# Two shifted copies of VectorE's exponentials in one instruction, in a kernel of two attention and two linear-attention layers

## The chip, the cores and the metric

The kernel runs on one core of a Trainium2 chip. A core has TensorE (PE, matrix multiplications into PSUM), VectorE (DVE), ScalarE (ACT), GpSimd (POOL), SyncE (SP, which here issues DMAs), an SBUF of 128 partitions and a PSUM of eight banks of 128x512 fp32. Each engine works through its own list of instructions in order and waits on semaphores for the others. The metric is the device time of one execution in microseconds (us), lower is better.

## What is computed

Four residual layers on one sequence of 2048 tokens of width 512, alternating between two kinds. Kind A is softmax attention with 32 query heads of width 16 and a single key and value head; kind B is linear attention with a feature map of exp.

```python
x = A_x                                             # 2048 x 512, bf16
x = x + A(layernorm(x), wq, wk, wv, wo)             # layer 0
x = x + B(layernorm(x), wqkv, wo)                   # layer 1
x = x + A(layernorm(x), wq, wk, wv, wo)             # layer 2, the weights of layer 0
x = x + B(layernorm(x), wqkv, wo)                   # layer 3, the weights of layer 1

A: scores = q k^T / 4;  p = softmax(scores);  out = (p v) wo
B: phi(t) = (t + 1 if t > 0 else exp(t)) + 1e-6
   o = phi(q) (phi(k)^T v) / (phi(q) sum(phi(k)) + 1e-6);  out = o wo
```

An A layer needs 32 x 2048 x 2048 exponentials, and these fill most of the time.

## The kernel before

**Tiles and segments.** Tokens come in 16 tiles of 128. In an A layer the work is cut into blocks: one block is the scores of 128 keys against 512 columns (a query tile of 128 tokens for four heads), which is one PSUM bank. A segment (`Seg`) is half of one query tile's heads against a range of key tiles; a layer has 2048 blocks in all. For each block TensorE makes the scores (L965, tile `ps<-QT,KM`, a matmul that uses 32 of the 128 rows, so that up to four run side by side), an engine takes the exponential out of PSUM into SBUF, and TensorE multiplies it by the values (L1019) into 32 columns of the accumulator bank `ACC`; four blocks of different column groups run side by side as one value group.

**Two engines take exponentials.** ScalarE takes the exact one (L1150, tile `PT`) of two or three banks at a time. There are two bank sets of three banks each: while ScalarE works on one, TensorE fills the other. VectorE takes an approximation (L1247, tile `FB`): scores come out of TensorE scaled so that adding a constant and writing as int16 gives the bits of a bf16 power of two. That is piecewise linear, and it is made smooth by averaging: the same bits plus 32, 64 and 96 (a quarter, a half and three quarters of an octave) make three more copies (L1289), and each of the four copies (`NSH = 4`) is multiplied with its own weighted values (`VW`, weights `WTS`). So a block of ScalarE's costs TensorE one value matmul, and a block of VectorE's costs four, plus its share of three copies on VectorE.

**Chunks and buffers.** VectorE collects up to `CHB = 4` blocks in one buffer of `FB`, a chunk of 2048 elements in each partition; `dve_close` then starts `dve_shifts`, which takes three more buffers, one after the other, and posts a copy for each. `FB` has 12 buffers (`NFB`). A buffer comes free when the copies that read it and the value matmuls on it are done (`hold`, `spend`). A new chunk is opened only with more than `FBO` buffers free (`dve_hit`), and a copy for a segment that isn't due yet waits while no more than `FBS` are free.

**Who gets a block.** A block goes to VectorE in one of three ways: as the third bank of a round (`dve_split`; ScalarE then takes two banks, and the set is given back when both engines are done with it), if VectorE has less than `BLS` us queued of some urgency and less than `BLT` in all; in a free bank beside a round (`dve_open`); or by itself when VectorE runs low (`alone`).

**The order.** No order is written by hand. A planner (`Planner`) runs the whole program once in Python, while the kernel is built, with an assumed duration and latency for every operation, and gives each engine the ready operation of the best priority whenever it is free. What comes out is a fixed list for each engine, with semaphore waits; only the lists run on the chip. The assumed durations are in the `op(...)` calls and in constants (`PV_DUR` 0.222 for a value group, `QK_LAT` 0.438 from the start of score matmuls to the exponential, `SWITCH` 0.107 between row and column use of TensorE, `EXO` 0.0625 plus 0.4267 a bank for an exponential, `EX_LAT` 0.185 from its end to whoever waits for it). One rule concerns TensorE: `yields` (L72 to L78) holds back an operation that isn't a score matmul when it would make the next score matmuls of a set late. `self.turns` has for each running exponential when it will be done and how late the score matmuls into its banks may start; an operation is held if it would end more than `HTOL` + `HK` x (time until the banks are free) after the later of the two. Where TensorE would be empty, `fill` (L1064) puts in matmuls on zeros.

```python
            if r < self.now + HMAX and self.now + dur - max(r, late()) > HTOL + HK * max(0.0, r - self.now):
                return max(r, self.now) + 0.005
```

```python
BLS = 1.6        # L428
FBO = 2          # L455
FBS = 4          # L456
HTOL = 0.02      # L485
```

Of the kernel before, what the change touches and what calls it, by code (L numbers as in the profile page):

```python
# [8 lines left out]
I16 = mybir.dt.int16  # L9
ACTF = mybir.ActivationFunctionType  # L10
ALU = mybir.AluOpType
# [413 lines left out]
FARO = 12  # L425
FARM = {1: range(4, 16), 3: ()}
GROW = (5,)
BLS = 1.6  # L428
BLO = 5.0
DXB = 1.4  # L430
BLT = 2.5
# [16 lines left out]
NSH = 4  # L448
WTS = (0.353515625, 0.296875, 0.25, 0.2099609375)
WLOG = 0.5565237382  # L450
EXPBIAS = (SHIFT + WLOG) * math.log(2.0)
VB = (127.0 + SHIFT) * 128.0
VLO = 16384.0
CHB = 4
FBO = 2  # L455
FBS = 4  # L456
AHEAD = 20
QUICK = (4, 12)
KFIRST = True
# [22 lines left out]
OWNP = 2.0  # L482
HMAX = 0.2
KSP = True
HTOL = 0.02  # L485
HK = 0.3
MCOP = (DV,)*4
EVP = 1.2
# [8 lines left out]
def bass_interleave_layers__grouped_kv_mqa__linear_attn_block__prompt_kernel(  # L497
# [458 lines left out]
    def run_a(L):  # L956
# [13 lines left out]
        def pv_post(src, blk, hold, w=None):  # L970
            def arrived():
                for sg, kt, j, ap, key in blk:
                    sg.ready.append((kt, j, ap, key, hold, w))
                pv_kick()
            if src.done:
                arrived()
            else:
                src.users.append(arrived)

        def spend(h, o):  # L980
            h[0] -= 1
            if o not in h[1]:
                h[1].append(o)
            if h[0] == 0:
                pl.give_after(h[2], h[3], h[1])
# [233 lines left out]
        def dve_hit(js):  # L1219
            if not chunk["blk"] and (len(fb_pool.free) <= FBO or fb_pool.wait):  # L1220
                return None
            hit = dve_pick(js)
            if hit is not None:
                if not chunk["blk"]:
                    chunk["f"] = fb_pool.free.pop(0)
                    chunk["hold"] = [NSH - 1, [], fb_pool, chunk["f"]]
                hit[0].need[hit[2]] += NSH - 1
                hit[0].total += NSH - 1
            return hit
# [43 lines left out]
            pl.process(dve_shifts(blk, chunk["f"], chunk["hold"]))  # L1273

        def dve_shifts(blk, f_, hold):
            n = 512 * len(blk)
            pr = 8.0 + 0.001 * min(x[0].i for x in blk)
            si = min(x[0].i for x in blk)
            for w in range(1, NSH):
                while len(fb_pool.free) <= FBS and sum(x.total - x.submitted for x in segs[cur["i"]:si]) > (AHEAD if segs[si].blocks < 32 else 0):  # L1280
                    yield ("sleep", 0.2)
                g_ = yield ("acq", fb_pool, pr)
                while PSH and len(blk) == CHB and pl.backlog(DV) > PBL and not all(o.done for o in pl.ws(("FB", f_, len(blk) - 1))):
                    yield ("sleep", 0.1)
                pool = PSH and len(blk) == CHB and not pl.busy[PO] and state["po"] == 0 and pl.backlog(DV) > PBL
                if pool:
                    state["po"] += 1
                en, du = (PO, n / 1165.0 + 0.25) if pool else (DV, n / 3840.0 + 0.068)
                o = op({en: (du, lambda e, w=w, g_=g_: e.tensor_scalar(  # L1289
                    out=FB[:, g_, 0:n].bitcast(I16), in0=FB[:, f_, 0:n].bitcast(I16), scalar1=float(w * 128 // NSH), scalar2=None, op0=ALU.add))},  # L1290
                       reads=[("FB", f_, h) for h in range(len(blk))], writes=[("FB", g_, h) for h in range(len(blk))], prio=pr, lat=0.15, port=True)
                if pool:
                    def gone():
                        state["po"] -= 1
                    o.users.append(gone)
                spend(hold, o)
                pv_post(o, [(sg, kt, j, FB[:, g_, h * 512:(h + 1) * 512], ("FB", g_, h)) for h, (sg, kt, j) in enumerate(blk)], [len(blk), [], fb_pool, g_], w)

        oslot = {}

# [581 lines left out]
```

## Time and profile before

| | us |
|---|---|
| median of three runs | 1488.83 (1487.35 to 1489.05) |
| the profiled execution | 1489.33 |
| its span, first instruction to last | 1487.6 |
| TensorE busy | 1433.2 (96%) |
| VectorE busy | 1439.2 (97%) |
| ScalarE busy | 1452.5 (98%) |

The views used are: the page's busy time of each engine; the chain of waits (followed back from the last instruction, at each step to what released it); the costliest groups of instructions (line, engine, operation, tile written <- tiles read, shapes, count | busy us, mean ns of one | idle time before them and what ended it); the waits (engine and line that waited <- what it waited for: us in total, times, longest); and the order of instructions in time (start, duration, engine, line; neighbours of one line are merged, with their count). A record lasts until its result is written and so overlaps the next record of its engine; the cost of an instruction to its queue is the distance from its start to the next one's. PEld is the loading of weights into TensorE, which a matmul starts with. The first A layer runs its exponentials from about 10 to 707 us, the second from about 700 to 1451 us, with layer 1 mostly between and beside them, and layer 3 at the end.

### The profile page before, as it was taken

The page shows a single profiled execution, that of the slowest core. Times are in us where ns is not written, and L with a number is a line of the kernel's source. Part 1 is how long each engine was busy: PE and PEld are TensorE (multiplying, and loading weights), DVE is VectorE, ACT ScalarE, POOL GpSimd, SP SyncE. Part 2 cuts the span into 40 slices and gives each one's busy share as a digit, 9 for nine tenths or more (in the row PEclk, how much of TensorE's full clock was granted, in tenths as well). Part 3 has the DMA queues.
Part 4 walks back from the last instruction along what each step waited for, and adds up shares of the span by engine and source line. Part 5 has one row for each costly group of instructions (what it writes and reads, how often), then busy time and mean ns, then how long its engine had stood idle before and what let it go on. Part 6 is the DMA issues. An engine that isn't in the chain of part 4 may idle for free.

```text
span 1487.6 us, 36547 instructions
## 1 busy us (share of the span) xinstructions
PE 1433.2 (96%) x14825; PEld 520.1 (35%) x14924; DVE 1439.2 (97%) x2686; ACT 1452.5 (98%) x1444; POOL 77.0 (5%) x155
## 2 busy tenths in 40 slices
PE   8999999999999999999999999999999999999998
PEld 5423333333333333333733333333333333333335
DVE  8999999999999999999878999999999999999996
ACT  8999999999999999999799999999999999999996
POOL 5000000000000000000011000000000000000000
PEclk9999999999999999999999999999999999999999
DMA  5200000000000000000031000000000000000001
GB/s 115 72 9 9 9 8 7 6 7 6 9 9 9 9 5 5 2 2 2 2 47 40 2 12 9 12 9 5 8 9 5 9 9 9 9 2 2 2 2 58
DMA packets 53542, 20.74 MB, mean 14 GB/s; under 512 B 47232, under 2 KB 52864, under 8 KB 53376
## 3 DMA queue, kind: packets, MB, share of 16 engines
q1 hardware_dynamic: 52320, 18.36, 5.7%
q8 instruction: 120, 1.97, 0.6%
q14 instruction: 46, 0.38, 0.1%
q10 hardware_dynamic: 1056, 0.03, 0.0%
HBM read 5.28 MB, written 2.10 MB: 5 GB/s over the span
## 4 chain that ended last, share of the span: by engine, by line
DVE 46%; PE 38%; ACT 7%; issue 7%; DMA 1%; POOL 0%; POOLq 0%; SPq 0%; ACTq 0%
DVE FB L1247 22%; DVE FB L1289 16%; PE ps L1019 13%; PE ps L965 11%; ACT PT L1150 7%; PE ps L711 5%; PE ps L1064 4%; PE ps L879 2%; PE ps L1334 1%; DVE sacc L1312 1%; DVE st L793 1%; DVE xn L802 1%; DVE QT L1422 1%; DVE Osb L1345 1%; DVE sacc L1422 1%
## 5 line engine op out<-in xcount | busy, mean ns | idle before, releaser
L1150 ACT ACTIVATE PT<-ps 128x1024 bf16<-128x1024 f32 (+1 forms) x1309 | 1400.1, 1309 | 5.6 <-PE ps L1019 2.7
L1247 DVE TENSOR_SCALAR FB<-ps 128x512 int16<-128x512 f32 x1047 | 689.0, 680 | 4.4 <-PE ps L965 3.1
L965 PE MATMUL ps<-QT,KM 32*128 32x512 bf16 x4096 | 525.6, 385 | 24.9 <-ACT PT L1150 16.9
L1019 PE MATMUL ps<-FB,VW 128*32 128x512 bf16 x4188 | 526.1, 384 | 8.3 <-DVE sacc L1312 5.3
L1289 DVE TENSOR_SCALAR FB<-FB 128x2048 int16<-128x2048 int16 (+1 forms) x789 | 517.6, 676 | 0.3
L1019 PE MATMUL ps<-PT,V 128*32 128x512 bf16 x3049 | 472.8, 386 | 0.4 <-issue 0.3
L965 PEld LDWEIGHTS ps<-QT,KM 32*128 32x128 bf16 x4096 | 133.0, 91 | 466.5 <-ACT PT L1150 381.7
L1064 PE MATMUL ps<-QT,V 128*32 128x512 bf16 (+6 forms) x927 | 249.8, 347 | 0.4
L1019 PEld LDWEIGHTS ps<-FB,VW 128*32 128x32 bf16 x4188 | 130.4, 94 | 163.3 <-issue 97.1
L1019 PEld LDWEIGHTS ps<-PT,V 128*32 128x32 bf16 x3049 | 114.7, 94 | 102.9 <-issue 74.5
L1064 PEld LDWEIGHTS ps<-QT,V 128*32 128x32 bf16 x927 | 79.8, 96 | 88.6 <-issue 32.9
L784 POOL TENSOR_TENSOR rs<-ve,mhalf 128x1 f32<-128x1 f32 x59 | 43.9, 745 | 578.9 <-DVE ve L782 576.6
L711 PE MATMUL ps<-wqkv,xnT 128*128 128x512 bf16 (+1 forms) x217 | 62.2, 367 | 7.0 <-issue 3.5
L1419 ACT ACTIVATE phE<-ps 128x512 bf16<-128x512 f32 (+1 forms) x66 | 45.8, 696 | 6.0 <-PE ps L879 5.0
L782 POOL TENSOR_SCALAR ve<-mv 128x1 f32<-128x1 f32 x32 | 14.9, 466 | 683.8 <-DVE mv L794 683.7
L1312 DVE COPY sacc<-ps 128x512 f32<-128x512 f32 x64 | 43.6, 681 | 3.3 <-PE ps L1019 3.2
L1334 PE MATMUL ps<-identF,sacc 128*128 128x128 f32 x256 | 46.3, 291 | 0.0
L793 DVE BATCH_NORM_STATS2 st<-x_sb 128x6 f32<-128x512 bf16 x60 | 40.5, 681 | 2.5 <-DMA x_sb<-in_A_x_dram 2.3
L879 PE MATMUL ps<-xnT,wqkv 128*128 128x128 bf16 x512 | 38.0, 220 | 0.0
L879 PE MATMUL ps<-xnT,wq 128*128 128x128 bf16 x464 | 35.2, 220 | 0.0
L1334 PEld LDWEIGHTS ps<-identF,sacc 128*128 128x128 f32 x256 | 27.3, 140 | 20.6 <-issue 11.8
L879 PEld LDWEIGHTS ps<-xnT,wqkv 128*128 128x128 bf16 x512 | 29.5, 98 | 9.8 <-issue 7.0
(139 smaller groups left out, 630.4 us busy)
## 6 DMA issues: line engine op xcount, KB each, us to landing
out_dram<-x_sb SPq DMA_DIRECT2D x16, 128.0 KB, 1.7
x_sb<-in_A_x_dram SPq DMA_DIRECT2D x6, 256.0 KB, 5.0
wqkv<-in_B_wqkv_dram SPq DMA_DIRECT2D x1, 1536.0 KB, 8.7
xnT<-xn SPq DMA_TRANSPOSE x48, 2.4
x_sb<-in_A_x_dram SPq DMA_DIRECT2D x4, 128.0 KB, 2.4
wq<-in_A_wq_dram SPq DMA_DIRECT2D x1, 512.0 KB, 4.5
wo<-in_A_wo_dram SPq DMA_DIRECT2D x1, 512.0 KB, 5.4
wo<-in_B_wo_dram SPq DMA_DIRECT2D x1, 512.0 KB, 9.4
```

The source lines that it names most:

```text
L711: return e.matmul(dst, lhsT=l, rhs=r, start=(k == 0), stop=(k == len(pairs) - 1))
L793: op({DV: (0.6, lambda e: e.bn_stats(st[:, t, 0, :], x_sb[:, t, :]))}, reads=[("x", t)], writes=[("st", t)], prio=prio, lat=0.13)
L879: ins = e.matmul(dst[:, g * P:(g + 1) * P], lhsT=lhs(g, k), rhs=rhs(k), start=(k == 0), stop=(k == FT - 1))
L965: return e.matmul(bank(b), lhsT=KM[r, sg.par, kt * P:(kt + 1) * P], rhs=QT[r, sg.t, :], start=True, stop=True)
L1019: ins = e.matmul(ps[32 * j:32 * j + 32, ACC * 512:(ACC + 1) * 512], lhsT=V[:, kt, :] if w is None else VW[:, kt, w, :], rhs=ap, start=(k = ...
L1064: o = op({PE: (n / 2400.0, lambda e: e.matmul(ps[32 * j:32 * j + 32, b * 512:b * 512 + n], lhsT=V0[:], rhs=QT[:, sg.t, 0:n], start=st, sto ...
L1150: ex = op({AC: (EXO + 0.4267 * n, lambda e, n=n, s_=s_, p_=p_: e.activation(PT[:, p_, 0:n * 512], ps[:, s_ * 512:(s_ + n) * 512], ACTF.Exp ...
L1247: o = op({DV: (0.602, lambda e: e.tensor_scalar(out=dst.bitcast(I16), in0=bank(b), scalar1=VB, scalar2=VLO, op0=ALU.add, op1=ALU.max))}, w ...
L1289: o = op({en: (du, lambda e, w=w, g_=g_: e.tensor_scalar(out=FB[:, g_, 0:n].bitcast(I16), in0=FB[:, f_, 0:n].bitcast(I16), scalar1=float(w ...
L1312: o = op({DV: (0.6, lambda e, src=src: e.tensor_copy(src, bank(ACC)))}, writes=[B_(ACC), key], prio=0.0, lat=0.15)
L1334: o = op({PE: (0.12, lambda e, c=c: e.transpose(ps[:, b * 512 + c * P:b * 512 + (c + 1) * P], src[:, c * P:(c + 1) * P], identF[:]))}, rea ...
L1419: op({AC: (0.07 + n / 1200.0, lambda e: e.activation(phE[:, i, 0:n], bank(b, n), ACTF.Exp))}, reads=[B_(b)], writes=[("phE", i)], prio=pr ...
```

## The change

The three copies of a chunk were three instructions, each reading the chunk's own buffer. Now the first instruction makes the copy shifted by one step (32) into a buffer `a_`, and a second instruction reads the two buffers `f_` and `a_` together, adds two steps (64), and writes two buffers `b_` and `c_`: the copies shifted by two and by three steps. The pattern over two buffers is a slice with a step, `FB[:, lo:hi + 1:hi - lo, 0:n]`, so the two need not be neighbours. Both `f_` and `a_` are held until this instruction is done, and `b_` and `c_` are taken at the same time. `wait` replaces the acquisition by priority: it polls every 0.1 us of the planner's time until enough buffers are free. An unused way to put copies on GpSimd (`PSH`) goes. Four constants change with it.

```diff
-BLS = 1.6
+BLS = 1.2
...
-FBO = 2
-FBS = 4
+FBO = 3
+FBS = 2
...
-HTOL = 0.02
+HTOL = .05
...
-                    chunk["hold"] = [NSH - 1, [], fb_pool, chunk["f"]]
+                    chunk["hold"] = [1, [], fb_pool, chunk["f"]]
...
-            for w in range(1, NSH):
-                while len(fb_pool.free) <= FBS and sum(x.total - x.submitted for x in segs[cur["i"]:si]) > (AHEAD if segs[si].blocks < 32 else 0):
-                    yield ("sleep", 0.2)
-                g_ = yield ("acq", fb_pool, pr)
...
-                en, du = (PO, n / 1165.0 + 0.25) if pool else (DV, n / 3840.0 + 0.068)
-                o = op({en: (du, lambda e, w=w, g_=g_: e.tensor_scalar(
-                    out=FB[:, g_, 0:n].bitcast(I16), in0=FB[:, f_, 0:n].bitcast(I16), scalar1=float(w * 128 // NSH), scalar2=None, op0=ALU.add))},
-                       reads=[("FB", f_, h) for h in range(len(blk))], writes=[("FB", g_, h) for h in range(len(blk))], prio=pr, lat=0.15, port=True)
...
-                spend(hold, o)
-                pv_post(o, [(sg, kt, j, FB[:, g_, h * 512:(h + 1) * 512], ("FB", g_, h)) for h, (sg, kt, j) in enumerate(blk)], [len(blk), [], fb_pool, g_], w)
+            def wait(least):
+                return len(fb_pool.free) < least or fb_pool.wait or (len(fb_pool.free) < least + FBS and
+                       sum(x.total - x.submitted for x in segs[cur["i"]:si]) > (AHEAD if segs[si].blocks < 32 else 0))
...
+            def add(out, in_, c, k, reads, writes):
+                return op({DV: (k * n / 3840.0 + 0.068, lambda e: e.tensor_scalar(out=out.bitcast(I16), in0=in_.bitcast(I16), scalar1=float(c * 128 // NSH), scalar2=None, op0=ALU.add))},
+                          reads=[("FB", g, h) for g in reads for h in range(m)], writes=[("FB", g, h) for g in writes for h in range(m)], prio=pr, lat=0.15, port=True)
+
+            while wait(1):
+                yield ("sleep", 0.1)
+            a_ = fb_pool.free.pop(0)
+            o = add(FB[:, a_, 0:n], FB[:, f_, 0:n], 1, 1, [f_], [a_])
+            held = [m + 1, [], fb_pool, a_]
+            pv_post(o, [(sg, kt, j, FB[:, a_, h * 512:(h + 1) * 512], ("FB", a_, h)) for h, (sg, kt, j) in enumerate(blk)], held, 1)
+            while wait(2):
+                yield ("sleep", 0.1)
+            b_, c_ = sorted(fb_pool.free[0:2])
+            fb_pool.free = fb_pool.free[2:]
+            lo, hi = min(a_, f_), max(a_, f_)
+            o = add(FB[:, b_:c_ + 1:c_ - b_, 0:n], FB[:, lo:hi + 1:hi - lo, 0:n], 2, 2, [f_, a_], [b_, c_])
+            spend(hold, o)
+            spend(held, o)
+            post(o, b_, 2 if f_ == lo else 3)
+            post(o, c_, 3 if f_ == lo else 2)
```

More of the change, by code (lines that the diff above doesn't have):

```diff
@@ L451 @@
 EXPBIAS = (SHIFT + WLOG) * math.log(2.0)
+assert NSH == 4
 VB = (127.0 + SHIFT) * 128.0
@@ L1275, in dve_shifts @@
         def dve_shifts(blk, f_, hold):
[L1276 to L1277 removed]
+            m = len(blk)
+            n = 512 * m
             si = min(x[0].i for x in blk)
[L1279 to L1297 removed]
```

3 lines of the change are left out of this document (added).

## The prediction

> **What bounds the kernel now.** I read the page first: busy shares, then the chain of waits, then the costliest groups.
>
> ```profile
> span 1487.6 us, 36547 instructions
> PE 1433.2 (96%) x14825; PEld 520.1 (35%) x14924; DVE 1439.2 (97%) x2686; ACT 1452.5 (98%) x1444; POOL 77.0 (5%) x155
> DVE 46%; PE 38%; ACT 7%; issue 7%; DMA 1%; POOL 0%; POOLq 0%; SPq 0%; ACTq 0%
> L1150 ACT ACTIVATE PT<-ps 128x1024 bf16<-128x1024 f32 (+1 forms) x1309 | 1400.1, 1309 | 5.6 <-PE ps L1019 2.7
> L1247 DVE TENSOR_SCALAR FB<-ps 128x512 int16<-128x512 f32 x1047 | 689.0, 680 | 4.4 <-PE ps L965 3.1
> L1289 DVE TENSOR_SCALAR FB<-FB 128x2048 int16<-128x2048 int16 (+1 forms) x789 | 517.6, 676 | 0.3
> L1064 PE MATMUL ps<-QT,V 128*32 128x512 bf16 (+6 forms) x927 | 249.8, 347 | 0.4
> ```
>
> Three engines are full. L1247 and L1289 are VectorE's exponentials and their shifted copies; L1150 is ScalarE's exponentials; L1064 is filler that TensorE runs when nothing else is wanted, so TensorE has room and the other two have little. The chain passes through VectorE far more often than through ScalarE, so VectorE looks like the engine to relieve. The chain of the first attention layer's steady part (100 to 700 us) and of the second's (765 to 1440 us) say the same:
>
> ```profile
> by line: DVE FB L1247 26.4%; DVE FB L1289 19.0%; PE ps L1019 14.6%; PE ps L965 11.7%; ACT PT L1150 7.0%; PE ps L1064 4.9%; issue 3.1%; PE ps L711 2.8%; DVE sacc L1312 1.9%; PE ps L1334 1.8%; DVE sacc L1422 0.8%; DVE va L705 0.8%; DVE Osb L1
> by line: DVE FB L1247 22.5%; DVE FB L1289 16.5%; PE ps L1019 12.5%; PE ps L965 11.1%; issue 10.6%; ACT PT L1150 6.7%; PE ps L1064 4.0%; PE ps L711 3.8%; DVE sacc L1312 1.1%; PE ps L879 1.0%; PE ps L1334 1.0%; DVE QT L1422 1.0%; DVE Osb L134
> ```
>
> But "7%" does not mean that ScalarE has time to spare. Records overlap their successors, so the cost of one instruction is the distance between starts, which the order of instructions in time shows (ScalarE alone, then VectorE alone; the row at 1449.91 is a piece of the chain of waits):
>
> ```profile
> 938.31 5.60 ACT L1150 ACTIVATE PT<-ps 128x1024 bf16<-128x1024 f32 x6
> 943.73 0.67 ACT L1419 ACTIVATE phE<-ps 128x512 bf16<-128x512 f32 x1
> 944.21 1.11 ACT L1150 ACTIVATE PT<-ps 128x1024 bf16<-128x1024 f32 x1
> ...
> 1448.58 4.32 ACT L1150 ACTIVATE PT<-ps 128x1536 bf16<-128x1536 f32 x3
> 1449.91 3.00 ACT PT L1150 x2
> ...
> 699.90 1.28 DVE L1289 TENSOR_SCALAR FB<-FB 128x2048 int16<-128x2048 int16 x2
> 701.10 1.28 DVE L1247 TENSOR_SCALAR FB<-ps 128x512 int16<-128x512 f32 x2
> 702.30 0.28 DVE L1420 TENSOR_SCALAR phE<-phE 128x512 bf16<-128x512 bf16 x1
> 702.50 0.68 DVE L1289 TENSOR_SCALAR FB<-FB 128x2048 int16<-128x2048 int16 x1
> ```
>
> A two-bank exponential costs (943.73 - 938.31)/6 = 0.903 us, a three-bank one 1449.91 - 1448.58 = 1.33, a 512-column one 944.21 - 943.73 = 0.48. VectorE's exponential and its 2048-element copy cost 0.60 each, a 512-element one of the same kind 0.20.
>
> ```profile
> L1150 ACT ACTIVATE PT<-ps 128x1024 bf16<-128x1024 f32 x371 | 377.7, 1174 | 0.3 <-PE ps L1019 0.3
> L1150 ACT ACTIVATE PT<-ps 128x1536 bf16<-128x1536 f32 x186 | 282.0, 1594 | 0.4 <-PE ps L1019 0.4
> L1419 ACT ACTIVATE phE<-ps 128x512 bf16<-128x512 f32 x19 | 13.6, 716 | 0.0
> L1150 ACT ACTIVATE PT<-ps 128x1024 bf16<-128x1024 f32 x432 | 434.4, 1180 | 0.3 <-PE ps L965 0.3
> L1150 ACT ACTIVATE PT<-ps 128x1536 bf16<-128x1536 f32 x196 | 296.4, 1593 | 1.3 <-PE ps L1019 1.3
> L1419 ACT ACTIVATE phE<-ps 128x512 bf16<-128x512 f32 x29 | 22.0, 759 | 0.2 <-DVE FB L1289 0.2
> ```
>
> These groups are the two steady parts, 600 and 675 us. ScalarE's starts alone need 371x0.903 + 186x1.33 + 19x0.48 = 591.5 us of the first and 432x0.903 + 196x1.33 + 29x0.48 = 664.7 us of the second. That leaves 8.5 and 10.3: in 1275 us ScalarE loses about 19 us, 1.5%. Nothing can shorten these parts by more, unless ScalarE gets less to do.
>
> **The change part by part.** The changed instruction lists count differently, because the planner decides anew.
>
> *VectorE.* From 0.60 and 0.20 a copy costs 0.26 ns an element and 0.067 us fixed. A copy of two buffers (4096 elements) then costs 1.133; the bounds are 1.133 (all of one fixed part saved) and 1.20 (nothing saved), and I take 1.133, since 512 and 2048 lie on one line. The list has 259 copies of 2048 and 259 of two buffers in place of 777: 466.2 - 259x(0.60 + 1.133) = 17.4 us less. Short chunks: nine copies of 1536 (0.466 by the same line) and three of 1024 (0.333) become one of 0.333 and one of 0.60, 4.3 less. Exponentials: 1038 for 1047, 5.4 less. Together VectorE sheds 27.1 us. On the chain these two lines have about 42% of the time (45.4% and 39.0% above), so the end would move by 0.42x27.1 = 11.4 us at most; the rest lies beside ScalarE and TensorE.
>
> Of 259 copies of two buffers 92 lie in adjacent buffers on both sides, and 167 go row by row (two rows of 2048). No instruction of this trace reads two rows at this rate. [...] The second copy reads what the first has just written and waits for it; only where the two follow directly is VectorE idle for that, some 40 places in the list by what precedes each, well under 0.1 us each, and I count nothing, as VectorE now has 27 us to hide it in.
>
> A longer instruction makes what comes behind it on VectorE wait up to 1.13 instead of 0.60, above all the emptying of the value accumulator (L1312), and TensorE's next value group behind that. The filler covers it on TensorE; without cover it is half of 0.53 at 64 places times the share of such copies in VectorE's time (about a fifth), some 3 us. I leave it at nothing and keep it in the range.
>
> *Buffers and gates.* A chunk now takes its last two buffers at once (of 12), holds its first two until the double copy, and opens only with more than 3 free (FBO 3); BLS 1.2 lets VectorE take the third bank of a round only with less queued. That is why it gets 9 blocks fewer, and ScalarE more: 894 two-bank and 423 three-bank exponentials and one of a single bank, for 878 and 431: 16x0.903 - 8x1.33 + 0.48 = +4.3 us on ScalarE. Nothing hides that but the 19 us. The finer polls (0.1) issue no instruction, and SP, POOL and the DMAs keep their lists.
>
> *HTOL, 0.02 to 0.05.* This is the part that I weigh most. `yields` holds back a value group that would delay the next score matmuls of a bank set beyond HTOL. By its own constants, a value group (0.222) that starts when an exponential is done (EX_LAT 0.185), with a two-bank exponential running on the other set, makes these matmuls late by 0.185 + 0.222 - (0.0625 + 0.8534 - 0.438 - 0.107) = 0.036: refused before, allowed now. The lists show it. Before, 10 rounds of score matmuls stand directly behind a value group that reads the exponential which also frees their banks, 6 of them with a two-bank exponential running; now 199 do, 123 with two banks running. What one costs the trace of before shows, since some happen there:
>
> ```profile
> PEld ps L1019 <- ACT PT L1150: 4.9, 12, 0.7
> ...
> 1363.11 1.11 ACT L1150 ACTIVATE PT<-ps 128x1024 bf16<-128x1024 f32 x1
> 1364.27 0.10 PEld L1019 LDWEIGHTS ps<-PT,V 128*32 128x32 bf16 x4 [0.29 <-ACT PT L1150]
> 1364.60 0.39 PE L965 MATMUL ps<-QT,KM 32*128 32x512 bf16 x4
> 1364.03 1.10 ACT L1150 ACTIVATE PT<-ps 128x1024 bf16<-128x1024 f32 x1
> 1365.05 1.45 ACT L1150 ACTIVATE PT<-ps 128x1536 bf16<-128x1536 f32 x1
> ...
> 16.26 1.06 ACT L1150 ACTIVATE PT<-ps 128x1024 bf16<-128x1024 f32 x1
> 17.21 1.45 ACT L1150 ACTIVATE PT<-ps 128x1536 bf16<-128x1536 f32 x1
> ...
> 1433.41 1.27 ACT L1150 ACTIVATE PT<-ps 128x1024 bf16<-128x1024 f32 x1
> 1434.58 1.02 ACT L1150 ACTIVATE PT<-ps 128x1024 bf16<-128x1024 f32 x1
> ```
>
> The exponential ends at 1364.22, the value group loads at 1364.27, the score matmuls follow 0.33 later, and ScalarE's next start is 1.02 after the last one instead of 0.903: 0.12 lost. Nine rounds of before have this shape; the first loses 0.05, the last 0.27, their mean is 0.15. Of the 19 us, other two-bank rounds lose 0.02 each. So 123 - 6 = 117 more rounds cost ScalarE 117x(0.15 - 0.02) = +15.2 us, against 0.036 in the planner's sum. Bounds: 117x(0.05 - 0.02) = 3.5 and 117x(0.27 - 0.02) = 29; I take the mean of the nine. Behind the waiting value group stand the score matmuls, and ScalarE waits for those: what was beside the path lies on it.
>
> *The sum.* ScalarE +4.3 + 15.2 = +19.5; VectorE's relief takes 11.4 off the waits in which ScalarE and TensorE stood behind VectorE: +8.1. The profiled execution took 1489.33 (its span of 1487.6 and 1.7 around it) and would take 1497.4; against the median shown, 1488.83, it is 1496.9, and I say 1497.
>
> **The rivals.** *VectorE is the bound and its relief wins.* The chain (46% to 7%) speaks for it, and so does the filler: the changed list has 868 for 927, 384,512 columns for 399,488, as if the planner found less empty TensorE time. It needs the value-first rounds to cost what the planner thinks, 117x0.036 = 4.2 us and that inside ScalarE's 19. Then -11.4 + 4.3 = -7.1: 1482. Against it: the nine rounds.
>
> *ScalarE's queue sets the whole end.* If VectorE's relief frees nothing that ScalarE waited for, all +19.5 stays: 1508. The point from which it decides: more than 15 us of before's 19 must be waits for TensorE, not VectorE. For it, the waits view: of the score matmuls' waits few end on VectorE,
>
> ```profile
> PEld ps L965 <- ACT PT L1150: 381.7, 1023, 1.2
> PEld ps L965 <- DVE FB L1247: 46.2, 115, 0.6
> ```
>
> against it, that value groups are late because their VectorE blocks were.
>
> *It cancels.* At half the price of a value-first round (7.6) the sum is 4.3 + 7.6 - 11.4 = +0.5: 1489.
>
> *The double copy doesn't run at the fast rate.* At half of it the 167 two-row copies cost 4096x0.52 ns + 0.067 = 2.2, 1.07 more each, +178 us: 1667. Only a new access pattern speaks for it; it is left outside the range.
>
> **How the numbers follow.** Forecast (slower, about 1497) 0.50; the full queue 0.13; cancels 0.12; VectorE's relief wins 0.23; slow mode 0.02. About 0.2%, 3 us, is what this kernel's measurement can tell from no change. Faster by more is the relief, 0.23; within is the cancelling, 0.12; slower is the rest, 0.65. The forecast's own range is 1491 to 1504 (half and one and a half of 15.2). The range for 8 in 10 reaches to the relief and to the full queue: 1481 to 1509.
>
> **What would show it.** Right: the two-buffer copy's starts 1.13 apart, VectorE with some 2% idle and well under 46% of the chain, ScalarE with more; value groups that wait for ScalarE some 200 times and not 12, and two-bank exponentials 0.15 apart from their floor behind them. Wrong: ScalarE's loss in the steady parts falls below 19 us, which would mean that a value-first round is absorbed by a round before it that was late too; or a double copy above 1.2.

## The result, and the profile after

| kernel | median of runs, us | profiled span, us | ratio to before, 95% interval |
|---|---|---|---|
| before | 1488.84 (1487.35 to 1489.05, 4 runs) | 1487.6 | |
| changed | 1498.12 (1497.25 to 1498.15, 4 runs) | 1496.4 | 1.0062 [1.0050, 1.0075] |

The changed kernel is 9.3 us slower, 1.1 over the forecast of 1497. The page of the changed kernel, in the parts shown of before (the last two lines are groups with shapes kept apart):

```profile
span 1496.4 us, 36075 instructions
PE 1440.3 (96%) x14752; PEld 519.5 (35%) x14842; DVE 1423.4 (95%) x2407; ACT 1461.5 (98%) x1454; POOL 77.9 (5%) x155
PE 48%; DVE 27%; ACT 17%; issue 7%; DMA 1%; POOL 0%; SPq 0%; ACTq 0%
L1151 ACT ACTIVATE PT<-ps 128x1024 bf16<-128x1024 f32 (+2 forms) x1318 | 1405.1, 1209 | 6.4 <-PE ps L966 2.8
L1248 DVE TENSOR_SCALAR FB<-ps 128x512 int16<-128x512 f32 x1038 | 680.7, 681 | 24.3 <-PE ps L966 22.1
...
L1290 DVE TENSOR_SCALAR FB<-FB 128x4096 int16<-128x4096 int16 x259 | 313.5, 1213 | 0.6
L1290 DVE TENSOR_SCALAR FB<-FB 128x2048 int16<-128x2048 int16 x260 | 175.6, 682 | 1.6
```

VectorE's busy time falls by 15.8 us, its share of the chain from 46% to 27%, and yet the span grows. The time that VectorE got back stands in the row L1248: its exponentials had 4.4 us of idle time ahead of them, now 24.3, of which 22.1 in waiting for score matmuls. No more blocks came to it (1038, before 1047). ScalarE's groups in the two steady parts, 100 to 700 and 765 to 1440 us:

```profile
L1151 ACT ACTIVATE PT<-ps 128x1024 bf16<-128x1024 f32 x377 | 366.9, 1072 | 1.1 <-PE ps L1020 0.3 <-PE ps L966 0.2
L1151 ACT ACTIVATE PT<-ps 128x1536 bf16<-128x1536 f32 x180 | 259.5, 1484 | 0.0
L1430 ACT ACTIVATE phE<-ps 128x512 bf16<-128x512 f32 x19 | 12.4, 651 | 0.0
L1151 ACT ACTIVATE PT<-ps 128x1024 bf16<-128x1024 f32 x431 | 422.0, 1077 | 0.8 <-PE ps L966 0.2 <-PE ps L1020 0.2
L1151 ACT ACTIVATE PT<-ps 128x1536 bf16<-128x1536 f32 x194 | 282.9, 1491 | 2.0 <-PE ps L1020 1.2 <-PE ps L966 0.7
L1430 ACT ACTIVATE phE<-ps 128x512 bf16<-128x512 f32 x28 | 18.7, 667 | 0.0
```

By the distances of starts, 377x0.903 + 180x1.33 + 19x0.48 = 589.0 of 600 us, and 431x0.903 + 194x1.33 + 28x0.48 = 660.7 of 675. ScalarE loses 11.0 and 14.3 us there, 25.4 together for 18.8 before: 6.6 more. With the 4.3 us that its list is longer this is 10.9, about the 9.3 of the result. So the question is why ScalarE loses more while VectorE stands idle. The waits view (engine, tile and line, what it waited for: total us, times, longest us):

```profile
PEld ps L966 <- ACT PT L1151: 261.4, 691, 1.4
PEld ps L966 <- DVE FB L1248: 79.5, 206, 1.0
PEld ps L1020 <- ACT PT L1151: 63.9, 201, 0.7
DVE FB L1248 <- PE ps L966: 22.1, 53, 1.0
```

The third line is what the prediction was built on: 201 value groups that wait for ScalarE, for 12 before. The second and fourth are what it had passed over: score matmuls wait for a bank that VectorE's exponential still holds, 79.5 us in 206 places with 1.0 at most, for 46.2, 115 and 0.6 before.

How a long instruction of VectorE's can reach ScalarE is read here from the order of instructions around 322 us (start, duration, engine; ScalarE alone, then VectorE, then TensorE):

```profile
321.21 2.51 ACT L1151 ACTIVATE PT<-ps 128x1024 bf16<-128x1024 f32 x2
322.11 1.61 ACT L1151 ACTIVATE PT<-ps 128x1536 bf16<-128x1536 f32 x1
323.85 1.02 ACT L1151 ACTIVATE PT<-ps 128x1024 bf16<-128x1024 f32 x1
...
321.02 1.22 DVE L1290 TENSOR_SCALAR FB<-FB 128x4096 int16<-128x4096 int16 x1
322.15 1.28 DVE L1248 TENSOR_SCALAR FB<-ps 128x512 int16<-128x512 f32 x2
323.35 0.68 DVE L1290 TENSOR_SCALAR FB<-FB 128x2048 int16<-128x2048 int16 x1
...
321.28 0.63 PE L966 MATMUL ps<-QT,KM 32*128 32x512 bf16 x4
321.84 0.58 PE L1065 MATMUL ps<-QT,V 128*32 128x512 bf16 x2
322.43 0.60 PE L1020 MATMUL ps<-PT,V 128*32 128x512 bf16 x5
322.66 0.60 PE L1020 MATMUL ps<-FB,VW 128*32 128x512 bf16 x7
323.10 0.38 PE L1065 MATMUL ps<-QT,V 128*32 128x512 bf16 x1
323.41 0.39 PE L966 MATMUL ps<-QT,KM 32*128 32x512 bf16 x3
```

The double copy starts at 321.02 and lets VectorE go at 322.15, 1.13 later. The score matmuls of 321.28 to 321.91 have filled a bank for VectorE while it runs, and the exponential that empties it starts only at 322.15; by the list, the score matmuls of the next round wait for that exponential. Its bank comes free after ScalarE's (the exponential from 321.21 is followed at 322.11). At 322.43 TensorE takes three value groups first, and the score matmuls come at 323.41. ScalarE's three-bank exponential of 322.11 could have been followed at 323.44 and is followed at 323.85: 0.41 lost. That the planner put the value groups first because of VectorE's bank is read from the order, not shown: when the score matmuls come, VectorE's first exponential has been done for half a microsecond, and the first of the three value groups is itself one of the 201 that waited for ScalarE.

### The profile page after: what moved, and what is told of

It is laid out like the page before. It is cut to its first block, busy times and chain, and to the rows that moved or that the text cites. A ratio compares the mean times of both kernels' runs of the same rounds, so it can differ in the third digit from the quotient of the medians.

```text
span 1496.4 us, 36075 instructions
## 1 busy us (share of the span) xinstructions
PE 1440.3 (96%) x14752; PEld 519.5 (35%) x14842; DVE 1423.4 (95%) x2407; ACT 1461.5 (98%) x1454; POOL 77.9 (5%) x155
## 3 DMA queue, kind: packets, MB, share of 16 engines
q10 hardware_dynamic: 1056, 0.03, 0.0%
## 4 chain that ended last, share of the span: by engine, by line
PE 48%; DVE 27%; ACT 17%; issue 7%; DMA 1%; POOL 0%; SPq 0%; ACTq 0%
PE ps L1020 18%; ACT PT L1151 16%; PE ps L966 14%; DVE FB L1248 13%; DVE FB L1290 8%; PE ps L1065 6%; PE ps L712 5%; PE ps L880 2%; PE ps L1345 2%; DVE sacc L1323 1%; DVE st L794 1%; ACT phE L1430 1%; DVE QT L1433 0%; DVE sacc L1325 0%; DVE x_sb L1402 0%
## 5 line engine op out<-in xcount | busy, mean ns | idle before, releaser
L1151 ACT ACTIVATE PT<-ps 128x1024 bf16<-128x1024 f32 (+2 forms) x1318 | 1405.1, 1209 | 6.4 <-PE ps L966 2.8
L1248 DVE TENSOR_SCALAR FB<-ps 128x512 int16<-128x512 f32 x1038 | 680.7, 681 | 24.3 <-PE ps L966 22.1
L1020 PE MATMUL ps<-FB,VW 128*32 128x512 bf16 x4152 | 504.3, 385 | 8.8 <-DVE sacc L1323 5.2
L1290 DVE TENSOR_SCALAR FB<-FB 128x2048 int16<-128x2048 int16 (+1 forms) x520 | 487.1, 946 | 2.2
L1020 PE MATMUL ps<-PT,V 128*32 128x512 bf16 x3058 | 452.8, 387 | 1.6 <-ACT PT L1151 0.2
L1020 PEld LDWEIGHTS ps<-FB,VW 128*32 128x32 bf16 x4152 | 126.0, 94 | 165.0 <-issue 85.2
L1020 PEld LDWEIGHTS ps<-PT,V 128*32 128x32 bf16 x3058 | 111.5, 94 | 122.7 <-issue 58.0
L1065 PEld LDWEIGHTS ps<-QT,V 128*32 128x32 bf16 x868 | 71.3, 95 | 104.1 <-issue 65.1
L1430 ACT ACTIVATE phE<-ps 128x512 bf16<-128x512 f32 (+1 forms) x66 | 41.6, 632 | 5.7 <-PE ps L880 4.7
L1345 PEld LDWEIGHTS ps<-identF,sacc 128*128 128x128 f32 x256 | 27.4, 140 | 25.4 <-issue 15.6
```

The costliest lines, as they stand in the source:

```text
L1020: ins = e.matmul(ps[32 * j:32 * j + 32, ACC * 512:(ACC + 1) * 512], lhsT=V[:, kt, :] if w is None else VW[:, kt, w, :], rhs=ap, start=(k = ...
L1065: o = op({PE: (n / 2400.0, lambda e: e.matmul(ps[32 * j:32 * j + 32, b * 512:b * 512 + n], lhsT=V0[:], rhs=QT[:, sg.t, 0:n], start=st, sto ...
L1151: ex = op({AC: (EXO + 0.4267 * n, lambda e, n=n, s_=s_, p_=p_: e.activation(PT[:, p_, 0:n * 512], ps[:, s_ * 512:(s_ + n) * 512], ACTF.Exp ...
L1248: o = op({DV: (0.602, lambda e: e.tensor_scalar(out=dst.bitcast(I16), in0=bank(b), scalar1=VB, scalar2=VLO, op0=ALU.add, op1=ALU.max))}, w ...
L1290: return op({DV: (k * n / 3840.0 + 0.068, lambda e: e.tensor_scalar(out=out.bitcast(I16), in0=in_.bitcast(I16), scalar1=float(c * 128 // N ...
L1345: o = op({PE: (0.12, lambda e, c=c: e.transpose(ps[:, b * 512 + c * P:b * 512 + (c + 1) * P], src[:, c * P:(c + 1) * P], identF[:]))}, rea ...
```

## The experiments

Twelve kernels, each timed in five rounds beside before on the same chip (before's medians 1487.6 to 1488.5). "ScalarE's starts" is the count of its exponentials by 0.903, 1.33 and 0.48, "lost" the rest of the distances between their starts and ScalarE's next one, both over the whole profiled execution (one execution of each kernel); "waits for VectorE" is the row of score matmuls' loads that wait for VectorE's exponentials: us, times, longest.

| kernel | last two copies | us | ratio to before | VectorE's blocks | ScalarE's starts + lost | waits for VectorE |
|---|---|---|---|---|---|---|
| before | separate | 1488.8 | 1 | 1047 | 1366.1 + 29.2 | 46.2, 115, 0.6 |
| changed | double | 1498.12 | 1.0062 | 1038 | 1370.4 + 35.4 | 79.5, 206, 1.0 |
| e1_htol02 | double | 1500.24 | 1.0079 [1.0067, 1.0092] | 1033 | 1372.4 + 31.6 | 70.4, 184, 1.0 |
| e2_before_htol05 | separate | 1489.31 | 1.0007 [0.9998, 1.0017] | 1045 | 1367.0 + 30.0 | 65.3, 184, 0.5 |
| e3_bls16 | double | 1504.92 | 1.0110 [1.0097, 1.0124] | 1050 | 1365.4 + 46.4 | 92.7, 253, 1.0 |
| e6_merge_only | double | 1496.07 | 1.0051 [1.0038, 1.0064] | 1050 | 1365.5 + 33.6 | 64.8, 176, 1.1 |
| e7_two_instr | separate | 1491.97 | 1.0028 [1.0018, 1.0038] | 1053 | 1363.5 + 25.5 | 49.9, 129, 0.6 |
| e9_gates | double | 1511.15 | 1.0155 [1.0140, 1.0169] | 1051 | 1364.9 + 41.8 | 67.5, 186, 0.9 |
| e10_fbo1 | double | 1499.97 | 1.0082 [1.0068, 1.0096] | 1069 | 1357.4 + 41.4 | 79.5, 209, 0.9 |
| e13_unit | unit of two | 1500.83 | 1.0087 [1.0073, 1.0101] | 1038 | 1370.5 + 30.7 | 79.0, 213, 1.1 |
| e14_merge_consts | double | 1488.55 | 1.0003 [0.9994, 1.0012] | 1056 | 1362.8 + 30.5 | 74.6, 196, 0.8 |
| e16_before_consts | separate | 1485.68 | 0.9985 [0.9976, 0.9994] | 1053 | 1363.7 + 27.7 | 46.8, 122, 0.7 |
| e17_merge_b | double | 1487.49 | 1.0000 [0.9991, 1.0009] | 1063 | 1359.9 + 32.2 | 88.1, 224, 0.9 |
| e19_unit_b | unit of two | 1494.36 | 1.0042 [1.0026, 1.0058] | 1050 | 1365.5 + 31.7 | 84.6, 218, 1.0 |

### HTOL: e1_htol02 and e2_before_htol05

The changed kernel without its HTOL, and before with it:

```diff
-HTOL = .05
+HTOL = 0.02
```

> The changed kernel with HTOL back at 0.02, all else as changed. Its list has 6 value-first rounds with a two-bank exponential running, not 123, and ScalarE 886 two-bank and 430 three-bank exponentials (894 and 423), a floor 2.1 us longer. Theory (HTOL's value-first rounds cost ScalarE about 0.07 each, the loss that the changed kernel's trace shows): 117 x 0.07 = 8 less, so 1498.1 - 8 + 2 = about 1492. Rival (the longer copy, the buffers and the gates cost the time): 1498 or more.

```diff
-HTOL = 0.02
+HTOL = 0.05
```

> The kernel before with HTOL 0.05 alone. Its list has 116 value-first rounds with a two-bank exponential running for 6, and nearly the same numbers for both engines' exponentials. Theory: ScalarE loses 110 x 0.07 to 0.15 = 8 to 16 more, so 1497 to 1505. Rival (HTOL does no harm by itself): 1489, within 3.

Measured: 1500.24 without it, which is not faster than with it (2.5 us slower by the ratios, within what two ratios leave open), and 1489.31 in before with it, no difference that can be told. The theory fell twice. It didn't fall for want of such rounds: the waits of before with HTOL .05, and its group of ScalarE's exponentials,

```profile
PEld ps L1019 <- ACT PT L1150: 61.7, 198, 0.5
...
L1150 ACT ACTIVATE PT<-ps 128x1024 bf16<-128x1024 f32 x877 | 863.9, 1090 | 2.3 <-PE ps L965 1.1 <-PE ps L1019 0.8
```

show 198 value groups that wait for ScalarE, about as many as in the changed kernel, at before's time. In the steady parts of that trace 102 two-bank exponentials run while a value group waits for ScalarE; they lose 10.9 us against 0.903, 0.11 each, and the 655 others lose 7.7 us, where in before 764 others lose 16.0. In the changed kernel 112 such rounds lose 9.4 us, 0.08 each, and 658 others 10.1, where without its HTOL (e1_htol02) 761 others lose 19.4. What one kind of round loses, the other gains, all but 2 us. The likely reason is that a value group that is done isn't in the way of later score matmuls; this wasn't shown place by place.

### The constants: e3_bls16 and e6_merge_only

The changed kernel with before's BLS alone, and with all four constants of before (BLS, FBO, FBS, HTOL), so that only the merge is left of the change:

```diff
-BLS = 1.2
+BLS = 1.6
```

> The changed kernel with BLS back at 1.6 alone. VectorE gets 1050 blocks for 1038 and ScalarE 918 two-bank and 403 three-bank exponentials, a floor 4.9 us shorter; 134 value-first rounds with two banks running, 11 more (0.8 us). Theory (ScalarE's floor and its losses set the end): 1498.1 - 4.9 + 0.8 = 1494. Rival (splitting less is what keeps ScalarE's sets from waiting for VectorE): slower than 1498.

```diff
-BLS = 1.2
+BLS = 1.6
-FBO = 3
-FBS = 2
+FBO = 2
+FBS = 4
-HTOL = .05
+HTOL = 0.02
```

> The double copy alone: the changed kernel with HTOL 0.02, BLS 1.6, FBO 2 and FBS 4. 10 value-first rounds, ScalarE's floor 0.5 us below before's, VectorE's exponentials 1050 for 1047 and 526 copies for 789: 16 us less for VectorE. Theory (the merge itself relieves VectorE, and HTOL was the cost): faster than before by 0.42 x 16 - 0.5 = about 7, 1482. Rival (the merge costs by longer instructions or by two buffers taken at once): 1489 or more.

Measured: 1504.92 and 1496.07. The merge alone costs 7.6 us (0.0051 of 1488); the four constants that came with it make up the other 1.6 together, which these two ratios can't tell from nothing. BLS 1.2 taken by itself, among the changed kernel's others, is worth 7 us to it. The 4.3 us of ScalarE's list are not what makes the merge slow: in the merge alone ScalarE's starts are 0.6 us below before, but it loses 4.4 more, and its other work between the first and the last exponential takes 50.0 us for 46.6. VectorE's groups in the merge alone,

```profile
L1248 DVE TENSOR_SCALAR FB<-ps 128x512 int16<-128x512 f32 x1050 | 683.4, 682 | 15.2 <-PE ps L966 13.2
L1290 DVE TENSOR_SCALAR FB<-FB 128x4096 int16<-128x4096 int16 x262 | 315.8, 1213 | 0.3
```

have 15.2 us of idle time ahead of the exponentials, for 4.4 before.

### Where in the merge: e7_two_instr, e9_gates, e10_fbo1

All three start from the merge alone. The first keeps its way of taking buffers, but makes the last two copies one by one; the second raises the gates that look at VectorE's queue; the third opens chunks with a buffer less free.

```diff
-            o = add(FB[:, b_:c_ + 1:c_ - b_, 0:n], FB[:, lo:hi + 1:hi - lo, 0:n], 2, 2, [f_, a_], [b_, c_])
+            o1 = add(FB[:, b_, 0:n], FB[:, lo, 0:n], 2, 1, [lo], [b_])
+            o = add(FB[:, c_, 0:n], FB[:, hi, 0:n], 2, 1, [hi], [c_])
```

> The kernel of the merge alone (1496.1 us, 7.6 over before), with its buffers taken as there, two at once and both held until the last copy, but with the second and third copy as two instructions of 2048 columns (0.60 us each) in place of one of 1.13 us. VectorE's 1053 exponentials and ScalarE's list (879 two-bank, 428 three-bank; floor 879 x 0.903 + 428 x 1.33 = 1363 us, 3 under before) are near those of before. Theory now: the cost is the long instruction, behind which an exponential of VectorE, and with it a bank and a value group, waits up to 1.13 us instead of 0.60: then this is 1486 to 1490. Rival: the cost is the way of taking buffers (two at once, one held for the next copy): then it stays at 1495 to 1500, or above, since the 3 to 4 us that the merge relieves VectorE of per hundred microseconds are gone too.

```diff
-DXB = 1.4
-BLT = 2.5
+DXB = 1.95
+BLT = 3.05
```

> The kernel of the merge alone (1496.1 us) with the two gates that compare VectorE's backlog raised by about the 0.55 us by which one double copy is longer than one single (1.4 to 1.95 for a block of VectorE's own, 2.5 to 3.05 for splitting a round); 915 two-bank and 405 three-bank exponentials on ScalarE, 1051 blocks on VectorE. If the list refuses VectorE blocks because one double copy in the queue looks like a full backlog, the idle time of VectorE's exponentials waiting for score matmuls (13.2 us in the merge alone, 3.1 before) falls under 8 and the time comes to 1488 to 1493. Rival: the gates are not what starves VectorE, and a longer backlog only makes more score groups wait behind a copy: 1497 to 1505.

```diff
-FBO = 2
+FBO = 1
```

> The kernel of the merge alone (1496.1 us) with one free buffer less asked for before VectorE opens a chunk; VectorE gets 1069 blocks instead of 1050, ScalarE's list becomes 938 two-bank and 383 three-bank exponentials, floor 938 x 0.903 + 383 x 1.33 = 1356 us, 9 under the merge alone. If the time follows ScalarE's floor (its losses stay at the 33.6 us of the merge alone): 1486 to 1490. Rival: VectorE's 19 more blocks (19 x 0.65 us and their copies) land where a long copy is ahead of them, so ScalarE's losses grow by as much or more: 1495 to 1502, with losses of 42 us and up.

(Relieving VectorE by 17.4 us is 1.2 us per hundred, not the 3 to 4 of the first expectation.) Measured: 1491.97, between the two theories; 1511.15; 1499.97. With two separate copies the signs of the merge vanish from the trace, in the waits

```profile
PEld ps L966 <- DVE FB L1248: 49.9, 129, 0.6
...
DVE FB L1248 <- PE ps L966: 4.3, 11, 0.8
...
ACT PT L1151 <- PE ps L1020: 5.5, 4, 3.7
```

and ScalarE loses 25.5 us, less than before. The 4 us by which this kernel is still over before lie outside ScalarE's exponentials: between its first and last one, 53.6 us go to other work and waits, for 46.6 before. Most of that is one place, the single wait of 3.7 us in the last line: an exponential of 512 columns starts at 909.48 and ScalarE's next one at 913.92, 4.44 later instead of 0.48. Between them TensorE's list has matmuls of a B layer (from 912.28, after 0.85 of waiting for VectorE). So the 4 us are a bad place of this list; that taking two buffers costs anything by itself isn't shown.

The other two came out on the side of their rivals, the gates beyond it. With FBO 1 VectorE took 19 blocks more, ScalarE's starts fell by 8.1 us, near the 9 expected, and its losses rose by 7.8: nothing was left. The 4.6 us (by the ratios) that it is slower than the merge alone lie outside the exponentials, 2.5 us between the first and the last and 2.0 behind the last. With the gates raised, VectorE's exponentials waited 21.2 us for score matmuls, not under 8, and ScalarE's losses rose by 8.2; half of the 15 us is one list's bad place, since

```profile
ACT PT L1151 <- PE ps L1020: 15.3, 9, 7.5
```

holds a single wait of 7.5 us, so this run says little about the gates themselves.

### Length or shedding: e13_unit

The merge does two things at once: it saves a fixed part of 0.07 us (1.13 for two copies of 0.60), and it takes away the point between two copies at which an exponential of VectorE could go. A unit of two ordinary copies, directly one after the other, does the second without the first. The edit, against e7_two_instr:

```diff
-            o1 = add(FB[:, b_, 0:n], FB[:, lo, 0:n], 2, 1, [lo], [b_])
-            o = add(FB[:, c_, 0:n], FB[:, hi, 0:n], 2, 1, [hi], [c_])
+            def two(e):
+                for g, s in ((b_, lo), (c_, hi)):
+                    ins = e.tensor_scalar(out=FB[:, g, 0:n].bitcast(I16), in0=FB[:, s, 0:n].bitcast(I16), scalar1=float(2 * 128 // NSH), scalar2=None, op0=ALU.add)
+                return ins
+            o = op({DV: (2 * n / 3840.0 + 0.135, two)}, ...
...
-            post(o1, b_, 2 if f_ == lo else 3)
+            post(o, b_, 2 if f_ == lo else 3)
```

> The kernel with two separate copies (1492.0 us), with these two issued as one unit: two instructions of 2048 columns directly one after the other, 1.20 us, between which no exponential of VectorE can go. VectorE's work for a chunk is that of before (three copies of 0.60 us), so nothing is shed, and it can be interrupted as rarely as with the double copy. ScalarE's list: 906 two-bank and 415 three-bank exponentials and one of 512, floor 906 x 0.903 + 415 x 1.33 + 0.5 = 1370.6 us. Theory now: what costs is the length for which VectorE takes no exponential, and the 17 us that the merge sheds give back a part: then this is over the merge alone (1496.1 us), at 1498 to 1503, 6 to 11 us over the two separate copies. Rival: what costs is the instruction over two buffers itself (its pattern, or that it needs both buffers and both copies' readers at once): then a unit of two ordinary instructions stays at 1490 to 1494.

Measured: 1500.83. The rival falls as far as it means the pattern over two buffers. Its other half stays open: by the last two lines of the edit the values of the first copy wait for the end of the unit, as in the double copy, and the length and this delay weren't taken apart. The groups and the waits of this kernel (L1306 is the unit's copies)

```profile
L1248 DVE TENSOR_SCALAR FB<-ps 128x512 int16<-128x512 f32 x1038 | 673.7, 679 | 15.5 <-PE ps L966 13.9
L1306 DVE TENSOR_SCALAR FB<-FB 128x2048 int16<-128x2048 int16 x518 | 329.4, 679 | 0.2
...
PEld ps L966 <- DVE FB L1248: 79.0, 213, 1.1
```

have every sign of the changed kernel with before's instructions: VectorE's exponentials waiting 13.9 us for score matmuls, score matmuls waiting 79.0 us for VectorE's exponentials, the longest 1.1. From two separate copies to the unit the ratio goes from 1.0028 to 1.0087, 8.8 us (13.0 from before itself, whose list lacks the bad place at 909 us); from the unit to the double copy down to 1.0051, 5.4 us.

### The same with other constants: e14_merge_consts, e16_before_consts, e17_merge_b, e19_unit_b

Other constants give other lists, and the table shows kernels with a double copy from 1487 to 1511 us by constants alone, so one pair of lists says little. The merge was tried with a second set, with three separate copies as in before, a double copy, and a unit. The set, against before's:

```diff
-BLS = 1.6
+BLS = 1.3
-DXB = 1.4
-BLT = 2.5
+DXB = 1.45
+BLT = 2.6
-ENDL = 12
+ENDL = 8
-FBO = 2
-FBS = 4
+FBO = 1
+FBS = 2
-HTOL = 0.02
+HTOL = 0.03
-CHT = 19
-CHS = 10
+CHT = 18
+CHS = 8
```

> The kernel before, three separate copies, with other constants (BLS 1.3 for 1.6, DXB 1.45 for 1.4, BLT 2.6 for 2.5, ENDL 8 for 12, FBO 1 for 2, FBS 2 for 4, HTOL 0.03 for 0.02, CHT 18 for 19, CHS 8 for 10). ScalarE's list: 891 two-bank and 420 three-bank exponentials and one of 512, floor 1363.7 us, 2.4 under before, with VectorE at 1053 blocks for 1047. If freed constants alone are worth something without the merge: 1484 to 1487, under both kernels. If not: 1488 to 1492.

> The double copy with exactly the constants of the run before it in this list (before with BLS 1.3, FBO 1, FBS 2, HTOL 0.03 and the rest), so that these two differ by the merge alone, a second pair beside before and the merge alone (+7.6 us). ScalarE's list: 933 two-bank and 389 three-bank exponentials, floor 1359.9 us. If the double copy costs more than it sheds whatever the constants: 3 to 9 us over that run, though ScalarE's floor is 3.8 us lower, by losses on ScalarE and idle time on VectorE in waiting for score matmuls. Rival: the 7.6 us were particular to before's constants, and the sheds count here: 0 to 4 us under it.

> The second set of constants again (BLS 1.3, FBO 1, FBS 2, HTOL 0.03 and the rest), with the last two copies as one unit of two instructions of 0.60 us in place of the double copy. ScalarE's list: 923 two-bank and 400 three-bank exponentials, floor 1365.5 us. This and the two runs with these constants (three separate copies 1485.7, double copy 1487.5) split the merge into its two sides: from separate copies to the unit nothing is shed and VectorE takes no exponential for 1.20 us; from the unit to the double copy only the 0.07 us each are shed. Theory: the length costs and the shedding pays with either set of constants, so 1493 to 1499. Rival: the 9 us between the unit and the separate copies with the first constants were particular to these lists: 1484 to 1490.

Measured: 1485.68, 1487.49 and 1494.36. Going to the unit costs 0.0057, 8.5 us, and from the unit to the double copy 0.0042, 6.2 us, come back. (Here the way of taking buffers changes together with the length; two separate copies with the new buffers weren't run with this set. The same step with before's constants is the 13.0 us from before to the unit.) Both steps have the sign that they had with before's constants; the shedding has about its size too, the length doesn't. The waits of the three, in this order:

```profile
PEld ps L965 <- DVE FB L1247: 46.8, 122, 0.7
```

```profile
PEld ps L966 <- DVE FB L1248: 88.1, 224, 0.9
```

```profile
PEld ps L966 <- DVE FB L1248: 84.6, 218, 1.0
```

The net of the two sides is small, 1.8 us, just under the 3 to 9 that were expected.

Where the two steps go, in us of the profiled executions:

| step | span | ScalarE's starts | lost | ScalarE's other work between first and last exponential | ahead and behind | VectorE's blocks |
|---|---|---|---|---|---|---|
| e7_two_instr to e13_unit | +8.8 | +7.0 | +5.2 | -3.5 | 0 | 1053 to 1038 |
| e13_unit to e6_merge_only | -4.9 | -5.0 | +2.9 | -0.1 | -2.7 | 1038 to 1050 |
| e16_before_consts to e19_unit_b | +8.7 | +1.8 | +4.0 | +2.7 | +0.1 | 1053 to 1050 |
| e19_unit_b to e17_merge_b | -6.4 | -5.6 | +0.5 | -1.6 | +0.3 | 1050 to 1063 |

(The -3.5 of the first row has in it the 4 us of the bad place at 909 us.) With the unit ScalarE loses 4 to 5 us more in both sets; the rest of that step is the planner's, which deals VectorE fewer blocks. The shedding comes back as 12 and 13 more blocks for VectorE, so ScalarE's starts need 5.0 and 5.6 us less. It doesn't come back as fewer losses.

The added waits can be placed. Of the 206 in the changed kernel, 84 (37.6 of the 79.5 us) are for an exponential that runs directly behind a double copy. Directly behind the unit it is 68 (28.4 us) in e13_unit and 87 (37.1 us) in e19_unit_b, about what each has more than its separate copies. The ScalarE exponentials that run while such a load waits lose 8.2 us in e13_unit and 6.7 in e19_unit_b, 5.9 in e6_merge_only and 4.4 in e17_merge_b, but only 2.0 in the changed kernel.

Last, the changed kernel with yet another set (FBO 1, FBS 4, HTOL 0.02, CHT 17):

```diff
-FBO = 3
-FBS = 2
+FBO = 1
+FBS = 4
-HTOL = .05
+HTOL = 0.02
-CHT = 19
+CHT = 17
```

> The changed kernel with the double copy as it is, and other constants: FBO 1 for 3, FBS 4 for 2, HTOL 0.02 for 0.05, CHT 17 for 19, which give another order. ScalarE's list: 921 two-bank and 399 three-bank exponentials and one of 512, floor 921 x 0.903 + 399 x 1.33 + 0.5 = 1362.9 us, 7.4 under the changed kernel; VectorE takes 1056 blocks for 1038. If the cost of the double copy is a tendency of the order that a fitting order avoids in part: 1487 to 1491. If it is fixed at each double copy (264 of them), it stays: 1495 to 1500.

Measured: 1488.55, level with before. So the cost isn't fixed at each double copy; a list that happens to fit makes it up, as constants move either form by several us. The fastest kernel of all has three separate copies: before with the second set, 1485.68, 0.15% under before [0.06%, 0.24%]. It beats before and the changed kernel, without the change.

## Why the prediction was right, and where it was wrong

**Right in sign and size (1497 for 1498.1), for a cause that was not the one priced highest.** That the size came out to 1 us is luck: the two dearest terms of the sum were wrong, and one that was left at nothing made up for them. Each difference below is of two ratios that are each known to about 0.0012, so it is known to 2 or 3 us. (Half of the 15.2 for HTOL puts the lower end of the forecast's own range at 1489, not at 1491; the result lies inside either way.)

**The bound** held. VectorE's relief was not worth its share, because ScalarE has no time to spare: ScalarE's exponentials account for the result (4.3 us longer list, 6.6 more lost in the steady parts). So does its reserve, "unless ScalarE gets less to do": that is how shedding paid where it did.

**VectorE's shedding** was right in cost and size, not in its way: the double copy costs 1.13 (322.15 - 321.02), as assumed. For two rows that lie apart no run showed this 1.133 beforehand: it was the author's estimate, drawn out from instructions on one row (0.20 for 512 elements, 0.60 for 2048). The changed kernel's trace shows it: behind 238 of the 259 double copies VectorE's next start comes within 1.14 for 4096 elements. By the list 41 of the 259 lie in adjacent buffers on both sides, not 92 (so many write adjacent buffers), and 103 on neither; the median distance is 1.13 for both kinds, and 94 of the 103 come within 1.14. Worth: the prediction gave the merge 17.4 us at 42%, so 7.3; the two pairs of unit and double copy measured 5.4 and 6.2. But it took the 42% off waits, and the measured gain is in blocks that ScalarE no longer has to take. Where the double copy directly follows the copy that it reads, 32 places, half start 0.12 later than the 0.60, 2 us in all; this was rightly left out.

**The step that failed, first: "117x(0.15 - 0.02) = +15.2 us" for HTOL.** The count was right (201 value groups wait for ScalarE) and the price was not. Such a round loses 0.08 and not 0.15, and the other two-bank rounds lose 9 us less (10.1 for 19.4 without HTOL). The price came from nine rounds of before, of which its own count has only 6 with two banks running; why these lose more isn't shown. Before with HTOL .05 has the 198 waits and before's time, so HTOL by itself costs nothing that can be told, for +15.2. "What was beside the path lies on it", the prediction says; it doesn't hold: the price of one kind of round was added without asking what the rest of the rounds would get back.

**The step that failed, second: the longer instruction, left "at nothing", with 3 us at most.** It named the emptying of the value accumulator as what would stand behind a double copy, 64 places. What stands directly behind the 259 double copies are VectorE's own exponentials, 191 times, and the emptying only 12 times; behind each exponential is a bank that the next score matmuls need. Separate copies against one unit cost 8.8 us (13.0 from before) and, with the second set, 8.5 us. That TensorE waits behind the long instruction is counted (84 places, 37.6 us, where separate copies have none), and in the units and the merge alone ScalarE loses 6 to 8 us at these places. In the changed kernel it loses 2.0 there, so by which way most of its 6.6 us arise stays open. The waits rank the kernels only roughly: before with HTOL .05 has 65.3 us of them with 0.5 at most, and e17_merge_b has the second most, 88.1 us, and both run in before's time.

**The buffers and gates** came out as counted in the list (+4.3 on ScalarE), but the merge doesn't need it to be slow: with before's constants ScalarE's starts are those of before and the merge still costs 7.6.

**The sum in its measured terms:** from three separate copies to the unit +13.0, shedding -5.4, the four constants (HTOL among them) +1.6: +9.2. As steps of one path these add up by construction. They stand in place of list +4.3, HTOL +15.2 and relief -11.4.

**The rivals.** VectorE's relief as the winner fell because the relief (5 to 6 us) is less than what the length costs. The full queue didn't apply, as the relief does come through, by way of blocks. The cancelling had HTOL's price a round about right, half, and like the forecast left the length at nothing. The double copy at half the rate, 2.2 us, was ruled out by 1.13; the half and its chance of 0.02 were the author's estimate.

**What was to show it** was only half a test: the double copy at 1.13, VectorE's share of the chain and the 200 waiting value groups were all there, and all but the first are there with HTOL alone, at no cost (198 groups; VectorE has 32% of the chain in before with HTOL .05). The sign of being wrong, losses under 19 us in the steady parts, didn't come (25.4), and yet what it stood for was so: the other rounds took up what the value-first rounds lost. The sign that told was one that wasn't named: VectorE's exponentials with 24.3 us of idle time ahead of them.

## What to carry to other kernels

An instruction on a shared engine had two prices here: its time, and the time for which nothing else can go (1.13 us for the double copy, 0.60 for a single one). Where the engine also serves a short loop (a bank that two other engines wait for), joining two instructions sheds a fixed part at every pair (0.07 us) and lengthens that loop (the longest of the waits for VectorE is 0.8 to 1.1 us in the kernels with a double copy or a unit, 0.5 to 0.7 with separate copies); ask first what is the most urgent thing in that engine's queue, and whether it can wait for the longest instruction. What is shed on a helper paid here where the helper took work over from the full engine (12 and 13 blocks, 5.0 and 5.6 us of ScalarE's starts), so count that work in the lists. Where lists are planned anew at every edit, one pair of lists can't price an edit of 0.5%: a single bad place was worth 4 us here, and 7.5 in another kernel. And when a rule moves waits from one kind of place to another, price the places that lose them too: try the constant alone, in the kernel before, ahead of explaining a difference by it.

## What the runs showed of the hardware that was not expected

The record of a two-bank exponential shrinks where value groups go first, 1.07 to 1.08 us in the changed kernel (1072 and 1077 ns in the steady parts) and 1.09 in before with HTOL .05, for 1.17 in before and 1.14 in the changed kernel's code with HTOL 0.02, while the median distance of starts is 0.904 in both before and the changed kernel. So the mean of a record on ScalarE says little of what an exponential costs here; where two overlap, the starts do. What makes the record longer wasn't tried.
